# Query loads with four tokens in a row per partition, in a chunked attention block that feeds a GELU MLP

## The chip, the core and the metric

The kernel runs on one core of a Trainium2 chip. The metric is the device time of one execution in microseconds (us). Three runs of the kernel before gave 198.75, 198.85 and 199.21 us, median 198.85 us. A difference of 0.2% of that is 0.4 us.

## The reference

Inputs are q, k and v of shape (4, 8, 768, 64): batch, heads, tokens, head dimension, all fp32, with one decay `lam` per head, and two MLP weights of 512 x 2048 and 2048 x 512. The attention walks over blocks of 64 tokens. The result of the attention is laid out as 3072 tokens of 512 features and goes through the MLP.

```python
for b in range(nb):                       # 12 blocks of 64 tokens
    intra = einsum('bhic,bhjc->bhij', qb, kb) * Dmask      # lam ** (i - j), i >= j
    intra = einsum('bhij,bhjd->bhid', intra, vb)
    inter = einsum('bhid,bhde->bhie', qb * lam_pow, kv_state)   # lam ** (i + 1)
    out[:, :, sl] = intra + inter
    kv_state = lam ** 64 * kv_state + einsum('bhsd,bhse->bhde', kb * rev_pow, vb)
x = out.transpose(0, 2, 1, 3).reshape(3072, 512)
result = gelu_tanh(x @ w_in) @ w_out
```

## The kernel before, in words

**Steps.** The attention is cut into 24 steps. A step is 256 tokens of 4 heads, of one batch row; even steps take heads 0 to 3, odd steps heads 4 to 7 of the same tokens. `load_step` (L60) brings q, k and v of a step in three DMAs of 256 KB: a partition p holds tokens 2p and 2p + 1 of each of the four heads, so each DMA packet is two tokens of 64 fp32 values, 512 bytes. In SBUF the order is (head, token of the pair, dimension). With this layout, the upper and the lower 64 partitions are the two halves (chunks, called `c`) of 128 tokens.

**Decays.** The block's decay is put on the operands: q is multiplied by `dq` (a power of lam by the token's place, from -63 upward within a chunk of 128 tokens) and v by `dv`, its reciprocal; the mask then only has to be 0 or 1. The powers are made once at the start: lam is spread over all partitions by a small transpose on TensorE (L207) and copied to `lam_bc` (L209); GpSimd raises it to `pos` (two `pow` instructions of 128 x 4, L216); VectorE makes the second token of each pair with `odd` (L224), and the reciprocals with `inverse` (L227). Seven squarings on VectorE (L221) give lam to the power of 128 for the state's decay, which four small copies on ScalarE (`chunk_decay`, L229) place into `lumask` and `lamu`.

**One step.** `cast_q` (L277) multiplies q by dq and writes fp16, on VectorE (on GpSimd for step 3). `cast_k` (L290) converts k on ScalarE. `scale_v` (L264) multiplies v by dv on GpSimd. Steps 0 to 7 are transposed on TensorE (`stage_t`, L309) and copied out of PSUM; in steps 0 to 3 ScalarE copies q's half and VectorE k's (L325, L326). From step 8 on `transpose_dma` (L299) does it with a DMA transpose on SP's queue. `scores` (L344) multiplies k with q into PSUM, `causal` (L356) multiplies by the mask on VectorE, `products` (L365) or `burst` (L415) forms the state update, the masked scores times v, and q times the state. `x_out` (L475) copies the result on ScalarE to `xT` in token order. `update` (L491) advances the state on VectorE and spreads it into `u` on GpSimd.

**The MLP** is cut into pieces by `queue_group` (L544), which wait in a list called `filler`. `fill(n)` runs the next n pieces, so the order of TensorE's work is written out by hand at the end of the function (L930 to L1132): attention steps with MLP pieces between them. Every instruction is pinned to its place in program order, and each engine works through its own instructions in order.

**Loads.** All loads but `lam` and v of step 0 are issued by SP, in one queue: steps 0 to 2, q and k of step 3, the first half of the first block of w_in (`load_win(0, 0)`, L88), v of step 3, the second half, the rest of w_in, w_out (L96), then steps 4 to 8. Later steps are loaded where the program says so. Each of the q, k, v buffers has four copies, so a load also waits until the step four before it has been used. DMA transposes and output stores share SP's queue with the loads.

**The start.** Until the MLP's first pieces can run, TensorE has little to do, and `idle` (L177) gives it dummy products. The first MLP pieces are `mm1_part` (L832, matmuls at L838). They run in an order that follows the arrival of the data: the first two feature blocks of x against the first half of w_in, then the second two against the second half, whose casts are at L108 on ScalarE and L110 on VectorE.

```python
    for s in range(3):
        load_step(s)
    load_step(3, "qk")
    load_win(0, 0)
    load_step(3, "v")
    load_win(0, 1)
```

Of the kernel before, what the change touches and what calls it, by code (L numbers as in the profile page):

```python
# [15 lines left out]
def kernel(  # L16
# [43 lines left out]
    def load_step(s, names="qkv"):  # L60
        b, r = divmod(s, 2 * NSB)
        sb, half = divmod(r, 2)
        ts = ld32.setdefault(s, [])
        for nm, src in (("q", q), ("k", k), ("v", v)):
            if nm not in names:
                continue
            t = ld.tile([P, HH, 2, D], FP32, tag=nm + "32", name=f"{nm}32_{s}")
            rows = src[b, half * HH : (half + 1) * HH, sb * SB : (sb + 1) * SB, :]
            queue = nc.scalar if (nm, s) == ("v", 0) else nc.sync
            pin(queue.dma_start(out=t[:].rearrange("p h j d -> p h (j d)"),  # L70
                                in_=rows.rearrange("h (p j) d -> p h (j d)", j=2)))
            ts.append(t)
# [104 lines left out]
    def idle(n, wide=0):  # L177

        t = ps_M.tile([P, 512], FP32, tag="M", name="idle")
        for dt, w in [(FP32, wide)] * (wide > 0) + [(mybir.dt.bfloat16, 512)] * n:  # L180
# [3 lines left out]
    pos = const.tile([P, H], FP32)  # L184
    nc.gpsimd.iota(pos[:], pattern=[[0, H]], base=-63, channel_multiplier=2,
                   allow_small_or_imprecise_dtypes=True)
    nc.gpsimd.tensor_scalar(pos[64:128], pos[64:128], 128.0, None, ALU.subtract)

    rel = otp.tile([P, 2, 2, 64], FP32, tag="o32", name="rel")
    nc.gpsimd.iota(rel[:], pattern=[[-1, 2], [1, 2], [2, 64]], base=0, channel_multiplier=-2,  # L190
                   allow_small_or_imprecise_dtypes=True)
    ident = const.tile([P, P], FP16)
# [14 lines left out]
    pin(nc.tensor.transpose(lam_ps[:], lam_in[:].to_broadcast([H, P]), ident32[:]))  # L207
    lam_bc = const.tile([P, H], FP32)
# [3 lines left out]
    dq = const.tile([P, H, 2], FP32)  # L212
    dv = const.tile([P, H, 2], FP32)
    halves = [slice(hf * HH, (hf + 1) * HH) for hf in range(2)]
    for hs in halves:
        pin(nc.gpsimd.tensor_tensor(dq[:, hs, 0], lam_bc[:, hs], pos[:, hs], ALU.pow))  # L216
    sq = [lam_bc] + [const.tile([P, H], FP32, name=f"sq{i}", tag=f"sq{i}") for i in range(7)]
    lamu = const.tile([P, H // 2], FP32)

    def square(i):  # L220
        pin(nc.vector.tensor_tensor(sq[i + 1][:], sq[i][:], sq[i][:], ALU.mult))  # L221

    def odd(hs):
        pin(nc.vector.tensor_tensor(dq[:, hs, 1], dq[:, hs, 0], lam_bc[:, hs], ALU.mult))  # L224

    def inverse(hs):
        pin(nc.vector.reciprocal(dv[:, hs], dq[:, hs]))  # L227
# [9 lines left out]
    for i in range(7):  # L237
        square(i)
    odd(halves[0])


# [10 lines left out]
    def decay(t, s):  # L252
        hs = halves[s % 2]
        return t[:, hs, :].unsqueeze(3).to_broadcast([P, HH, 2, D])

# [21 lines left out]
    def cast_q(s):  # L277
# [4 lines left out]
        pin(q_eng.tensor_tensor(wide(tq), q32[:], decay(dq, s), ALU.mult))  # L282
        if s == 0:
            inverse(halves[0])
            odd(halves[1])
            inverse(halves[1])
# [22 lines left out]
    def stage_t(s):  # L309
# [7 lines left out]
        for i, t in enumerate((tq, tk)):  # L317
            to = Tps[i] if s < 4 else Tps[:, i]
            for hp in range(2):
                for j in range(2):  # L320
                    pin(nc.tensor.transpose(to[:, j, hp, :], t[:, j, 2 * hp : 2 * hp + 2, :],
                                            ident[:]))
# [18 lines left out]

    Ss = {}

    def scores(n):  # L344
        o = qkT[n]
        Sps = [ps_M.tile([P, 2, 2, P], FP32, tag="M", name=f"S{hl}") for hl in range(2)]
        for hp in range(2):
            for jk in range(2):
                for hl, c in TILES:
                    pin(nc.tensor.matmul(  # L350
                        Sps[hl][half64(c), hp, jk, :], o[half64(hl), 1, jk, hp, half64(c)],
                        o[half64(hl), 0, :, hp, half64(c)], start=True, stop=True,
# [12 lines left out]
    def products(n, s, banks=None, evacuate=True):  # L365
# [37 lines left out]
        for c in range(2):  # L403
# [3 lines left out]
            for hp in range(2):  # L407
                pin(nc.tensor.matmul(OK[c][:, hp * P : hp * P + P], u[:, hp].rearrange("p l d -> p (l d)"),  # L408
                                     o[:, 0, :, hp, half64(c)], start=False, stop=True,
# [5 lines left out]
    def burst(ns, ss, *mix, ahead=None):  # L415
# [39 lines left out]
        for i, s in enumerate(ss):  # L455
            for c in range(2):
# [3 lines left out]
                for hp in range(2):  # L460
                    pin(nc.tensor.matmul(O[c][:, i, hp, :], u[:, hp].rearrange("p l d -> p (l d)"),  # L461
                                         qTs[i][:, 0, :, hp, half64(c)], start=False, stop=True,
# [12 lines left out]
    def x_out(s, OK, second=None):  # L475
# [5 lines left out]
        for c in range(2):  # L481
            d = dst[:, :, c * P : (c + 1) * P].rearrange("p hp (t j) -> p hp j t", j=2)
            o = OK[c][:, 0:256].rearrange("p (hp j t) -> p hp j t", hp=2, j=2)
# [447 lines left out]
    prep(0)  # L931
    stage_t(0)
    chunk_decay()
# [227 lines left out]
```

## Time and profile before

| What | Value |
|---|---|
| median of three runs | 198.85 us (198.75 to 199.21) |
| the profiled execution | 198.79 us |
| its span in the profile | 197.0 us, so 1.79 us lie around the span |
| TensorE (PE) busy | 191.2 us, 97% |
| VectorE (DVE), ScalarE (ACT), GpSimd (POOL) busy | 149.0, 121.1, 74.4 us |
| DMA packets | 62,810, of 38.13 MB |
| granted TensorE clock | full speed throughout |
| q load | 24 issues of 256 KB, median 4.9 us from issue to landing |

PE is the TensorE matmul queue, PEld its weight loads, SP the engine that only issues DMAs. "L70" is line 70 of the kernel; a line such as `L70` may stand for several loads, so they are told apart by tile. The profile's chain of work goes back from the last instruction to whatever released each one. Busy time of PE includes the dummy products of the first microseconds, and says nothing by itself on whether a stage could start sooner.

### The profile page before, as it was taken

How to read it: one execution, taken by the hardware profiler on the slowest of the kernel's cores; microseconds unless marked ns; L12 is line 12 of the kernel's file. 1: busy time of each engine (PE TensorE's matmuls, PEld its weight loads, DVE VectorE, ACT ScalarE, POOL GpSimd, SP SyncE). 2: the span in 40 equal slices, each digit the busy share in tenths (PEclk: the TensorE clock that was granted, in tenths of full speed). 3: DMA queues.
4: the chain of work that ended last, by engine and by line, in shares of the span. 5: the costliest groups of instructions: out<-in, count | busy, mean ns of one | idle time of the engine just before them, and what ended most of it. 6: DMA issues, size and time to landing. Idle time of an engine off the chain costs nothing.

```text
span 197.0 us, 5913 instructions
## 1 busy us (share of the span) xinstructions
PE 191.2 (97%) x2431; PEld 140.1 (71%) x2431; DVE 149.0 (76%) x291; ACT 121.1 (61%) x249; POOL 74.4 (38%) x85
## 2 busy tenths in 40 slices
PE   8979999999999999999999999999999999999993
PEld 2556544446888888654688764578888888888882
DVE  4797722889999889859999927999656987487620
ACT  3663878357874685686845378844867746679221
POOL 6594213457554931169754517165002030002000
PEclk9999999999999999999999999999999999999999
DMA  5999999999999999999996998400211300020205
GB/s 167 292 324 384 387 383 386 300 285 297 259 220 248 257 333 231 213 238 288 226 294 132 274 310 202 92 7 0 53 67 42 107 6 2 0 110 29 77 19 198
DMA packets 62810, 38.13 MB, mean 194 GB/s; under 512 B 18624, under 2 KB 55744, under 8 KB 62784
## 3 DMA queue, kind: packets, MB, share of 16 engines
q1 hardware_dynamic: 62240, 37.50, 74.3%
q8 instruction: 19, 0.31, 0.7%
q10 hardware_dynamic: 544, 0.26, 0.5%
q14 instruction: 7, 0.06, 0.1%
HBM read 27.26 MB, written 6.29 MB: 170 GB/s over the span
## 4 chain that ended last, share of the span: by engine, by line
PE 89%; SPq 4%; DMA 4%; ACT 0%; issue 0%
PE Hps L561 25%; PE MX L640 18%; PE MY L640 9%; PE HX L739 7%; PE O2ps L576 7%; PE MW L640 4%; DMA wi<-in_moe_w_in_dram 4%; SPq L70 4%; PE HY L739 4%; PE S L350 3%; PE Hps L838 3%; PE HW L739 2%; PE OK L408 2%; PE O L461 1%; PE O L436 1%; PE OK L399 1%
## 5 line engine op out<-in xcount | busy, mean ns | idle before, releaser
L561 PE MATMUL Hps<-xT,w_in 128*128 128x512 f16 (+1 forms) x288 | 50.5, 332 | 0.0
L513 POOL TENSOR_TENSOR u<-t,lumask 128x256 f16<-128x256 f32 x40 | 30.9, 788 | 40.7 <-DVE t L506 27.0
L561 PEld LDWEIGHTS <-w_in 128*128 128x128 f16 x288 | 27.9, 98 | 19.1
L565 ACT ACTIVATE gT<-Hps 128x512 f16<-128x512 f32 x56 | 33.5, 598 | 11.6 <-PE Hps L561 11.1
L360 DVE TENSOR_TENSOR PT<-S,mask 128x512 f16<-128x512 f32 x48 | 30.3, 680 | 7.8 <-PE S L350 7.8
L266 POOL TENSOR_TENSOR v<-v,dv 128x512 f16<-128x512 f32 x24 | 28.7, 1197 | 15.2 <-DMA v<-in_v_dram 14.0
L640 PEld LDWEIGHTS <-gs 128*128 128x128 f16 x320 | 31.2, 98 | 3.6
L640 PEld LDWEIGHTS <-gT 128*128 128x128 f16 x240 | 23.3, 98 | 3.2 <-ACT gT L565 0.2
L640 PE MATMUL MX<-w_sum,gs 128*128 128x256 f16 x160 | 21.4, 273 | 0.0
L692 POOL TENSOR_TENSOR o<-u,q 128x512 f32<-128x512 f32 (+1 forms) x5 | 6.3, 1252 | 36.7 <-ACT u L657 36.7
L282 DVE TENSOR_TENSOR qk<-q,dq 128x512 f16<-128x512 f32 x23 | 19.1, 833 | 0.8 <-DMA q<-in_q_dram 0.7
L295 ACT ACTIVATE qk<-k 128x512 f16<-128x512 f32 x23 | 14.4, 625 | 7.4 <-DMA k<-in_k_dram 7.3
L610 DVE TENSOR_TENSOR gs<-gT 128x1024 f16<-128x1024 f16 (+1 forms) x24 | 16.9, 711 | 1.6 <-ACT gT L565 1.6
L576 PE MATMUL O2ps<-w_out,gT 128*128 128x512 f16 x64 | 14.6, 379 | 0.0
L487 ACT ACTIVATE xT<-OK 128x256 f16<-128x256 f32 x26 | 9.9, 452 | 7.0 <-PE OK L408 6.5
L739 PEld LDWEIGHTS <-ws 128*128 128x128 f16 x128 | 12.5, 98 | 1.6 <-issue 0.2
L487 ACT ACTIVATE xT<-O 128x256 f16<-128x256 f32 x22 | 8.0, 461 | 5.8 <-PE O L461 4.9
L657 ACT ACTIVATE u<-MX 128x256 f32<-128x256 f32 x18 | 6.9, 384 | 7.4 <-PE MX L640 7.3
L576 PEld LDWEIGHTS <-gT 128*128 128x128 f16 x64 | 6.1, 98 | 6.6
L350 PEld LDWEIGHTS <-qkT 64*64 64x64 f16 x384 | 6.0, 106 | 6.8 <-issue 3.6
L640 PE MATMUL MY<-w_out,gs 128*128 128x256 f16 x80 | 10.7, 273 | 0.0
L753 DVE COPY u<-HX 128x512 f32<-128x512 f32 x8 | 5.5, 688 | 6.8 <-ACT gT L757 4.3
(98 smaller groups left out, 318.4 us busy)
## 6 DMA issues: line engine op xcount, KB each, us to landing
q<-in_q_dram SPq DMA_DIRECT2D x24, 256.0 KB, 4.9
k<-in_k_dram SPq DMA_DIRECT2D x24, 256.0 KB, 5.0
v<-in_v_dram SPq DMA_DIRECT2D x23, 256.0 KB, 5.2
out_dram<-o SPq DMA_DIRECT2D x23, 256.0 KB, 4.3
wo<-in_moe_w_out_dram SPq DMA_DIRECT2D x4, 1024.0 KB, 9.4
wi<-in_moe_w_in_dram SPq DMA_DIRECT2D x4, 512.0 KB, 7.1
wi<-in_moe_w_in_dram SPq DMA_DIRECT2D x2, 1024.0 KB, 12.5
v<-in_v_dram ACTq DMA_DIRECT2D x1, 256.0 KB, 4.3
```

What stands on the lines that cost most here:

```text
L266: pin(nc.gpsimd.tensor_tensor(wide(tv[:]), ld32[s][2][:], decay(dv, s), ALU.mult))
L282: pin(q_eng.tensor_tensor(wide(tq), q32[:], decay(dq, s), ALU.mult))
L295: pin(nc.scalar.activation(out=wide(tk), in_=k32[:], func=AF.Copy))
L360: pin(nc.vector.tensor_tensor(t[:, hl].rearrange("p b c d -> p b (c d)"), Sps[:].rearrange("p b c d -> p b (c d)"), mask[:].unsqueeze(1).t ...
L487: pin(nc.scalar.activation(out=d, in_=o, func=AF.Copy))
L513: pin(nc.gpsimd.tensor_tensor(u[:], state[half][:].unsqueeze(2).to_broadcast([P, 2, 2, D]), lumask[:, 2 * half : 2 * half + 2, :].unsqueez ...
L561: pin(nc.tensor.matmul(by_block(Hps[:, i, :]), w_in16[:, c, f * P : (f + 1) * P], x(c), start=(c == 0), stop=(c == NC - 1)))
L565: pin(nc.scalar.activation(out=dst, in_=Hps[:], func=AF.Gelu_apprx_tanh))
L576: pin(nc.tensor.matmul(O2[tau][0][:], gT[:, f % HF, f // HF, tau * P : (tau + 1) * P], w_out16[:, f, :], start=(n == 0), stop=(n == NF - 1)))
L610: pin(nc.vector.tensor_tensor(g_rows(m, i), g_rows(a, i), g_rows(b, i), op))
L640: pin(nc.tensor.matmul(dst, lhsT, rhs, start=(opens and i == 0), stop=(closes and i == HF - 1), skip_group_check=True))
L739: pin(nc.tensor.matmul(dst[:, i, :], w_in_block(a, slice(c, c + 1), slice(f * P, f * P + P))[:, 0], x_block(b, slice(c, c + 1))[:, 0], sta ...
```

## The change

q is no longer loaded two tokens to a partition, but four. Its tile becomes (2 heads, 4 tokens, 64), and it is loaded in two DMAs of 64 partitions each: partitions 0 to 63 get heads 0 and 1 of the step, partitions 64 to 127 heads 2 and 3, with tokens 4p to 4p + 3. A packet is 1 KB, a DMA 128 KB. k and v stay as they were.

The rest follows from the new order. `dq` becomes (half, head pair, 4 tokens) and needs lam per partition half (`lam_q`) and its own position column `pos_q`; `dv` is no longer a reciprocal of dq but has a `pow` of its own with `pos_v`, and a multiplication by 1/lam. The mask's `iota` (a ramp of integers) follows the new order of queries. `stage_t` transposes the q tile in its new blocks; `queries` picks the columns of a chunk as four runs of 32 instead of two of 64; `x_out` writes its columns four apart instead of two apart. The seven squarings, which stood in one row ahead of the first `cast_q`, are spread: one before it, three after it, and three after `stage_t(0)`. The second half's `pow` for dv and the multiplication behind it go to GpSimd, after step 0's v.

```diff
+            if nm == "q":
+                t = ld.tile([P, 2, 4, D], FP32, tag=nm + "32", name=f"{nm}32_{s}")
+                for hp in range(2):
+                    pin(nc.sync.dma_start(
+                        out=t[64 * hp : 64 * hp + 64].rearrange("p l j d -> p l (j d)"),
+                        in_=rows[2 * hp : 2 * hp + 2].rearrange("l (p j) d -> p l (j d)", j=4)))
+                ts.append(t)
+                continue
...
-    nc.gpsimd.tensor_scalar(pos[64:128], pos[64:128], 128.0, None, ALU.subtract)
...
+    for i in range(1, 4):
+        r = slice(32 * i, 32 * i + 32)
+        pin(nc.vector.tensor_scalar(pos_q[r], pos_q[r], 128.0 * i, None, ALU.subtract))
+    pin(nc.vector.tensor_scalar(pos_v[64:128], pos_v[64:128], 128.0, None, ALU.add))
...
+    for hp in range(2):
+        r = slice(64 * hp, 64 * hp + 64)
+        pin(nc.vector.tensor_copy(out=lam_q[r], in_=l4[r, :, hp, :]))
...
-    for hs in halves:
-        pin(nc.gpsimd.tensor_tensor(dq[:, hs, 0], lam_bc[:, hs], pos[:, hs], ALU.pow))
+    def pow_q(hf):
+        pin(nc.gpsimd.tensor_tensor(dq[:, hf, :, 0], lam_q[:, hf, :], pos_q[:].to_broadcast([P, 2]),
+                                    ALU.pow))
+    def pow_v(hs):
+        pin(nc.gpsimd.tensor_tensor(dv[:, hs, 0], lam_bc[:, hs], pos_v[:].to_broadcast([P, HH]),
+                                    ALU.pow))
+    pow_q(0)
+    pow_v(halves[0])
+    pow_q(1)
...
+    def later_q(hf):
+        pin(nc.vector.tensor_tensor(dq[:, hf, :, 1], dq[:, hf, :, 0], lam_q[:, hf, :], ALU.mult))
+        pin(nc.vector.tensor_tensor(dq[:, hf, :, 2:4], dq[:, hf, :, 0:2],
+                                    lam_q2[:, hf, :].unsqueeze(2).to_broadcast([P, 2, 2]), ALU.mult))
+    def later_v(hs, eng):
+        pin(eng.tensor_tensor(dv[:, hs, 1], dv[:, hs, 0], inv[:, hs], ALU.mult))
...
-    for i in range(7):
-        square(i)
-    odd(halves[0])
+    pin(nc.vector.tensor_tensor(lam_q2[:], lam_q[:], lam_q[:], ALU.mult))
+    square(0)
+    later_q(0)
...
         if s == 0:
-            inverse(halves[0])
-            odd(halves[1])
-            inverse(halves[1])
+            pin(nc.vector.reciprocal(inv[:], lam_bc[:]))
+            later_v(halves[0], nc.vector)
+            later_q(1)
+            for i in range(1, 4):
+                square(i)
...
+    def queries(o, r, hp, c):
+        return o[r, 0].rearrange("p a b t -> p (a b) t")[:, :, 64 * hp + 32 * c : 64 * hp + 32 * c + 32]
...
-            d = dst[:, :, c * P : (c + 1) * P].rearrange("p hp (t j) -> p hp j t", j=2)
+            d = dst[:, :, c * P : (c + 1) * P].rearrange("p hp (t j) -> p hp j t", j=4)
...
     prep(0)
+    pow_v(halves[1])
+    later_v(halves[1], nc.gpsimd)
     stage_t(0)
+    for i in range(4, 7):
+        square(i)
     chunk_decay()
```

## The prediction

> **What bounds the kernel now.** I read the slices first, then the chain of waits in order of time, then the stages in which the chain was not on TensorE. A time is called measurable here if it differs by over 0.2%, 0.4 us. In the page's slices (PE: TensorE busy, DMA: busy share of the 16 DMA engines, in tenths):
>
> ```profile
> PE   8979999999999999999999999999999999999993
> DMA  5999999999999999999996998400211300020205
> ```
>
> After the start TensorE has no gap, so from about 20 us to 193.8 us the time is fixed matmul work; but the DMA engines are full over the first half as well. What decides the start is in the chain (start us, us, what):
>
> ```profile
> 8.47 0.83 SPq L94
> 9.35 0.47 SPq L70
> 9.81 0.04 issue
> 9.86 7.88 DMA wi<-in_moe_w_in_dram
> 17.74 0.02 issue
> 17.77 0.42 ACT w_in L108
> 18.19 0.05 issue
> 18.24 1.13 PE Hps L838 x8
> ...
> 41.61 0.12 PE OK L385 x8
> 41.73 0.33 PE Tps L321 x4
> 42.06 0.03 issue
> 42.09 0.40 PE Tps L321 x4
> ```
>
> TensorE's unbroken work starts at 18.24 us, behind the second half of the first w_in block, which landed at 17.74 us. Ahead of it in SP's queue stand q of steps 0 to 3. And at 42.09 us the transposes of step 5's k start 0.03 us late: ScalarE converts that k at 41.40 to 42.03 after waiting 3.5 us for its DMA. So a later stream of loads meets the path a second time there, with six q loads before it. The stages by microsecond (last columns: granted clock, DMA share, GB/s):
>
> ```profile
> 10.00:11.00 1.00, 1.00 (x46) 0.67 (x35) 1.00 (x2) 0.74 (x2) 1.00 (x2) 1.00 1.22 290
> 16.00:17.00 1.00, 1.00 (x12) 0.86 (x10) 1.00 (x3) 0.10 (x1) 0.53 (x1) 1.00 1.05 385
> 17.00:18.00 1.00, 0.89 (x22) 0.53 (x20) 0.49 (x2) 0.23 (x1) 0.51 (x1) 1.00 1.06 391
> ```
>
> The engines' DMA share is over 1 in each. The q, k, v packets of 512 B move at 290 GB/s, the w_in packets of 2 KB at 385 to 391. The third number after the comma is VectorE: full from 7 to 17 us. It is the second chain of the start:
>
> ```profile
> 4.54 0.15 DVE L224 TENSOR_TENSOR dq<-dq,lam_bc 128x4 f32<-128x4 f32 x1
> 6.77 0.42 DVE L326 COPY qkT<-Tps 128x512 f16<-128x512 f16 x1 [0.96 <-PE Tps L321]
> 15.97 1.28 DVE L360 TENSOR_TENSOR PT<-S,mask 128x512 f16<-128x512 f32 x2
> 17.77 0.43 DVE L110 CAST w_in<-wi 128x512 f16<-128x512 f32 x1 [0.51 <-DMA wi<-in_moe_w_in_dram]
> ```
>
> Its only slack before 18 us is 0.51 us ahead of the last line and about 0.1 us near 12.5 us.
>
> **What the Trainium skill says.** "SBUF — State Buffer", Door 1: The DMA port swizzle: partitions 0 to 63 reach 8 of the 16 DMA ports; it gives 196 GB/s measured for 64 partitions at 1 MiB, against 328 for 128, and a ceiling of about 218 GB/s. The same page, "Can I just issue two DMAs to hit both halves?": no, two such DMAs together gained 6% over one. No load of before has 64 partitions, so its trace can't tell. "DMA: Bandwidth & Descriptors", Why small descriptors are slow (HBM only): a fixed cost per packet, some 3 cycles beside 32 B per cycle. The trace agrees in sign and shows more: 2-KB packets are 1.33 times as fast as 512-B ones.
>
> **The change part by part.**
>
> *Packets.* 256 KB at 290 GB/s take 0.904 us, 32 packets on each engine, 28.2 ns a packet. At 388 GB/s they take 0.676 us, 8 packets, 84.5 ns. A straight line between them (9.4 ns plus 0.0367 ns per byte) puts a 1-KB packet at 47.0 ns; 16 of them are 0.752 us. So by packets alone a q load gains 0.15 us.
>
> *Half the partitions.* If each half is held to the page's rates, 256 KB take 1.20 us at 218 GB/s or 1.34 us at 196: 0.30 to 0.43 us more. The two halves stand back to back in the same engines' queues between full-width loads; one engine may already write the other half, or k, while its partner finishes, which gives some of it back. I take +0.2 us per q load, inside the bounds -0.15 and +0.43, and nearer to the slow one since the page's two-DMA test found little overlap. This number is the prediction.
>
> *Where it counts.* Four q loads stand before the w_in half of 17.74 us: +0.8 us at 18.24 us, whole, since TensorE waits for this DMA already. Six stand before step 5's k: +1.2 us at 42.09 us, of which 0.8 is paid; cover there is 0.03 us, so the rest, 0.4, is paid too. Step 6's k (landed 43.7 us, transposed at 45.23) has over 0.5 us of cover, step 7's (46.3 us, transposed at 50.17) 3 us. Later steps go through DMA transposes that land 2 to 5 us ahead of their scores, but for step 16: issued at 88.2 us, landed about 92.7, scores near 93.9. There the slower q loads and one more issue in front can cost 0 to 0.5 us; I take 0, as the queue's delay does not add up over the steps where SP waits for casts (24.2 us in its waits).
>
> *Issues.* 24 more on SP, 0.45 to 0.5 us each. Ahead of the w_in half it is four, 2.1 us. They hide: from 3.97 us on SP's issues of 0.5 us are stretched to 0.8 to 1.6 us by full queues, 2.7 us in all before 9.86. Step 0's k is issued 0.53 us later (1.78 us instead of 1.25); behind it in the queue the engines still have q and v of step 0, so its landing (5.35 us) moves by the q load's cost, not by 0.53. Without that cover it would cost up to 0.5 us at the first transpose.
>
> *The setup.* VectorE gains four tiny position subtractions and additions before 1.5 us, where it waits (one GpSimd instruction of 0.33 us goes away). After lam's transpose come two copies for lam_q ahead of lam_bc, about 0.1 us each. GpSimd then has three `pow` before step 0's v, not two. A `pow` of 128x4 takes 1.02 us; a subtraction of 64x8 takes 0.33, so I read 0.3 fixed and 0.18 per column: 0.66 us for the new 128x2, bounded by 0.4 and 1.02. They end at 3.4 + 0.66 + 1.02 + 0.66 = 5.7 us, before 5.85 where v was scaled: no cost. The first q cast keeps its 4.7 us (squares no longer stand ahead of it; the second `later_q` does). Then VectorE does reciprocal, `later_v`, two of `later_q` and three squares from 5.2 to 6.7 us, hidden in the 0.96 us wait before 6.77. The last three squares (0.195 us each from start to start, 0.59 us) fall behind that copy, into the full stretch: every VectorE step to 17 us moves by 0.6. ScalarE's four `chunk_decay` copies wait for the last square, until 7.8 instead of 6.83, and behind them in its queue k of step 1 is converted at 8.65, not 7.71; its transposes move by 0.6, which VectorE's delay covers. At the end 0.6 meets a slack of 0.51 on VectorE; on TensorE scores of step 3 (15.37), eight MLP pieces and the state product move by 0.6 and end at 18.45 instead of 17.89. With unchanged DMA, the MLP's second part would start at 18.45: +0.2 us. With DMA 0.8 later it costs nothing.
>
> *Layouts.* `stage_t`, `queries`, the mask and the casts keep their counts and columns. Runs of 64 cost nothing today (eight 128-column products of q and state take 0.55 us, four 0.33: 55 ns each), so runs of 32 are put at 0. A strided `x_out` takes 0.45 us against 0.38 for a plain 128x256 copy; the wider stride may add 0 to 0.07 us, 48 times on ScalarE, which is idle 39% of the time; in the start, four in a row (14.43 to 16.11) have 0.5 us before their use. Zero.
>
> *Sum.* 0.8 + 0.4 = +1.2 us, on the profiled execution's 198.79 (span 197.0 plus 1.79 around it), which lies 0.06 below the median: 200.0 us.
>
> **Rivals.**
> (a) VectorE and ScalarE set the start: `pow` costs 1.02 whatever its width, so the third ends at 6.45; VectorE stands at `later_q(1)` and all squares and the copy of 6.77 come 0.6 later, 1.2 in all. Less the slack, +0.8 at 18.24 us, with q loads about as before: 199.6. For it: VectorE full from 7 to 17 us. Against: a per-element price for `pow` is more natural.
> (b) Offset: ports don't bind, q loads gain 0.15 us, and the w_in half lands 0.6 earlier; but the setup's 0.2 takes the place of the wait, and steps 4 and 5 no longer wait. +0.1: 198.9.
> (c) Faster: the same gain, and the moved squares fall into gaps. The w_in half would land at 17.1 us; TensorE could then start as soon as its own queue allows, at 17.89 instead of 18.24, 0.35 us earlier, and a little is won at 42 us: 198.4. It decides from the point where q loads take under 0.85 us and the added VectorE work under 0.1 us net.
> (d) The loads don't become 1-KB packets: the page would show 62,810 packets again instead of 62,810 - 24 x 256 = some 56,700. The slices of the access pattern speak against it.
>
> **Chances.** Forecast (q loads 0.05 to 0.43 us dearer: 199.1 to 201.4): 0.55. (a) 0.15, (b) 0.17, (c) 0.13 (with (d) under 0.01 inside them). Range 198.4 to 201.0: about 0.1 is left out above (page's full price and a stall at step 16) and 0.1 below. The forecast's own range is 199.1 to 201.4. Faster by over 0.2% is (c), 0.13; within is (b) and the forecast's mildest end, 0.21; slower is the rest, 0.66.
>
> **What would show it.** In the stages from 5 to 12 us: GB/s under 290 shows the ports, over 300 the packets. The first w_in half-block should land near 18.5 us and the L838 matmuls behind it start near 19.0. Step 5's k should be waited for by ScalarE until about 42.5. VectorE's second cast of q should start near 7.7, and `chunk_decay` near 7.8. If L838 restarts at or before 18.3 us, the q load's price is wrong; if it is late while the w_in half landed at 17.7, (a) holds; if TensorE shows a new wait near 93 us, the later part is wrong.

## The result, and the profile after

The changed kernel takes 206.87 us against 198.82 us of the kernel before on the same chip: ratio 1.0398, 95% interval 1.0343 to 1.0453, slower by about 8 us. The forecast was 200.0 us, range 198.4 to 201.0. Of its six executions (205.28 to 210.11 us), two count as slow, being over 1.5% above the fastest (208.63 and 210.11 us); they are left out of the median and the ratio, and slow executions of the experiments below likewise. The profiled execution took 208.63 us (span 206.8), so the lags read from it run up to 9.8 us rather than 8.

The page's slices (5.2 us each) and its line on packets:

```profile
PE   8597999998899999969999999999999999999993
PEclk9979999999999999999999999999999999999999
DMA  4999999999999999999999998970022200020205
...
DMA packets 57053, 38.14 MB, mean 184 GB/s; under 512 B 19009, under 2 KB 49985, under 8 KB 57025
```

The packets are close to the forecast (57,053 against some 56,700), so q does arrive in 1-KB pieces. But TensorE now has a hole in the second slice, a granted clock of 0.7 in the third, and a hole near 90 us, the 6 in PE's row. The stages (last columns: granted clock, DMA share, GB/s):

```profile
4.00:5.00 1.00, 1.00 (x3) 0.27 (x2) 0.33 (x2) 0.00 (x0) 1.00 (x2) 1.00 0.81 163
6.00:7.00 1.00, 0.40 (x4) 0.23 (x4) 0.86 (x5) 0.00 (x0) 0.20 (x1) 1.00 1.13 187
10.00:11.00 1.00, 1.00 (x2) 0.51 (x3) 1.00 (x3) 0.93 (x5) 0.00 (x0) 0.50 1.21 233
17.00:18.00 1.00, 0.94 (x22) 0.47 (x19) 1.00 (x3) 1.00 (x2) 0.80 (x2) 1.00 1.11 381
```

From 10 to 11 us the same engines that moved 290 GB/s before move 233, with the same share of 1.2. From 4 to 5 us they are not even full. The w_in packets (17 to 18 us) move at 381 GB/s, near the 385 to 391 of before: whatever slows the loads is tied to the q, k, v stream. TensorE's own lines, in order of time (start us, us, then the idle time before it and what ended it):

```profile
8.48 0.40 PE L363 MATMUL Tps<-ident,qk 128*128 128x128 f16 x4 [1.68 <-ACT qk L336]
...
19.59 2.02 PE L882 MATMUL Hps<-xT,w_in 128*128 128x256 f16 x16
21.54 0.32 PE L429 MATMUL OK<-v,qk 64*64 64x64 f16 x16
21.80 0.94 PE L882 MATMUL Hps<-xT,w_in 128*128 128x256 f16 x7
```

The first wait is not at the w_in half but at the transposes of step 0's k: 6.10 us before, 8.48 now. Before, they were the last four of this line, which also holds the four of q:

```profile
5.67 1.06 PE L321 MATMUL Tps<-ident,qk 128*128 128x128 f16 x8
```

The L882 line of 21.80 us is the MLP's second part that stood at 18.24; it has no wait of its own in front, it comes after late work. But the w_in half is late too: it landed at 20.80 us, 17.74 before, and ScalarE's casts of it ended near 21.5 us, under 0.3 us before TensorE came to it. Further on there are two more waits, at k of step 5 (42.09 us before) and at a piece of the MLP's second product (80.94 before), each in its own stretch of TensorE's timeline:

```profile
47.34 0.40 PE L363 MATMUL Tps<-ident,qk 128*128 128x128 f16 x4 [0.71 <-ACT qk L336]
```

```profile
89.86 1.03 PE L684 MATMUL MX<-w_sum,gT 128*128 128x256 f16 x8 [1.75 <-ACT u L701]
```

The second of these lines was, in the kernel before:

```profile
80.94 1.04 PE L640 MATMUL MX<-w_sum,gT 128*128 128x256 f16 x8
```

ScalarE shows what it stands behind in the changed kernel:

```profile
88.91 0.63 ACT L336 ACTIVATE qk<-k 128x512 f16<-128x512 f32 x1 [3.15 <-DMA k<-in_k_dram]
89.44 0.37 ACT L701 ACTIVATE u<-MX 128x256 f32<-128x256 f32 x1
```

A late k load holds ScalarE in its conversion for 3.15 us; the copy `u` (here a partial sum of the MLP), next in ScalarE's order, has nothing to do with k but waits too, and TensorE with it. The lag of the same matmul against the kernel before is 2.4 us at step 0's k, 3.6 at the MLP's second part, 4.0 until 39 us, 5.3 at 42, 7.0 at 62, 8.9 at 81 and 9.8 at the end.

### The profile page after: what moved, and what is told of

Read it like the earlier page. It is cut to its first block, busy times and chain, and to the rows that moved or that the text cites. A ratio compares the mean times of both kernels' runs of the same rounds, so it can differ in the third digit from the quotient of the medians.

```text
span 206.8 us, 5967 instructions
## 1 busy us (share of the span) xinstructions
PE 193.9 (94%) x2429; PEld 140.5 (68%) x2431; DVE 150.3 (73%) x300; ACT 131.2 (63%) x249; POOL 73.4 (35%) x88
## 2 busy tenths in 40 slices
DMA packets 57053, 38.14 MB, mean 184 GB/s; under 512 B 19009, under 2 KB 49985, under 8 KB 57025
## 4 chain that ended last, share of the span: by engine, by line
PE 49%; DMA 26%; DVE 12%; ACT 5%; SPq 4%; issue 2%; DVEq 0%; ACTq 0%
PE MX L684 14%; PE Hps L605 10%; DMA k<-in_k_dram 8%; DMA q<-in_q_dram 8%; DMA wi<-in_moe_w_in_dram 7%; PE HX L783 6%; PE MY L684 6%; DVE gs L654 4%; DMA v<-in_v_dram 3%; PE HY L783 3%; PE MW L684 3%; SPq L72 2%; DVE PT L404 2%; ACT xT L531 2%; PE S L394 2%
## 5 line engine op out<-in xcount | busy, mean ns | idle before, releaser
L557 POOL TENSOR_TENSOR u<-t,lumask 128x256 f16<-128x256 f32 x40 | 30.0, 764 | 38.9 <-DVE t L550 30.1
L609 ACT ACTIVATE gT<-Hps 128x512 f16<-128x512 f32 x56 | 32.2, 605 | 6.9 <-PE Hps L605 6.4
L684 PEld LDWEIGHTS <-gT 128*128 128x128 f16 x240 | 23.3, 98 | 5.1 <-issue 1.9
L531 ACT ACTIVATE xT<-OK 128x256 f16<-128x256 f32 x26 | 17.1, 792 | 6.8 <-PE OK L452 5.2
L736 POOL TENSOR_TENSOR o<-u,q 128x512 f32<-128x512 f32 (+1 forms) x5 | 5.8, 1165 | 36.7 <-ACT u L701 36.7
L531 ACT ACTIVATE xT<-O 128x256 f16<-128x256 f32 x22 | 13.9, 805 | 4.8 <-PE O L505 4.2
L684 PE MATMUL MX<-w_sum,gT 128*128 128x256 f16 x80 | 10.4, 272 | 1.7 <-ACT u L701 1.7
L550 DVE SCALAR_TENSOR_TENSOR t<-t,lamu,OK 128x64 f32<-128x64 f32 x36 | 8.4, 275 | 3.7 <-ACT xT L531 1.5
```

The lines of the kernel that those rows point to most:

```text
L531: pin(nc.scalar.activation(out=d, in_=o, func=AF.Copy))
L557: pin(nc.gpsimd.tensor_tensor(u[:], state[half][:].unsqueeze(2).to_broadcast([P, 2, 2, D]), lumask[:, 2 * half : 2 * half + 2, :].unsqueez ...
L609: pin(nc.scalar.activation(out=dst, in_=Hps[:], func=AF.Gelu_apprx_tanh))
L684: pin(nc.tensor.matmul(dst, lhsT, rhs, start=(opens and i == 0), stop=(closes and i == HF - 1), skip_group_check=True))
```

## The experiments

Each edit is made in the kernel before, unless it says otherwise; times are medians, ratios against the kernel before on the same chip, brackets behind a ratio its 95% interval.

### The parts alone

*The load.* Only q's load becomes two DMAs of 64 partitions.

```diff
+                for hp in range(2):
+                    pin(nc.sync.dma_start(out=t2[64 * hp : 64 * hp + 64],
+                        in_=rows[2 * hp : 2 * hp + 2].rearrange("l (p j) d -> p l (j d)", j=4)))
```

> The kernel before, with only q's load changed: two DMAs of 64 partitions, 1-KB packets, into the same tile (the four heads' values then stand in another order, so the queries are mixed up; all else is as before). Theory A, the half-width loads are the cause: over half of the 8.7 us, 204 to 206 us, with the first w_in half landing some 2.5 us later than before and waits for q and k near 42 us. Theory B, the four-apart columns of the output copy are the cause: 200.0 to 200.5 us, as I forecast for the load. Theory C, the moved setup is the cause: under 200.5 us too.

Measured: 207.02 us, ratio 1.0409 (1.0366 to 1.0452), +8.2 us. This one part costs as much as the whole change. The first w_in half landed at 19.65 us, 1.9 later than before (2.5 expected). Two stages of the steady stream of loads:

```profile
41.00:42.00 1.00, 1.00 (x7) 0.41 (x6) 0.67 (x1) 0.15 (x1) 0.17 (x1) 1.00 1.21 195
...
44.00:45.00 1.00, 1.00 (x6) 0.29 (x3) 0.38 (x2) 0.00 (x0) 0.71 (x1) 1.00 1.19 211
```

The mean from 40 to 52 us, first in the kernel before, then with the load alone:

```profile
40.00:52.00 12.00, 11.97 (x193) 7.79 (x192) 10.95 (x22) 8.63 (x16) 8.50 (x9) 1.00 1.13 290
```

```profile
40.00:52.00 12.00, 11.10 (x130) 5.86 (x127) 7.78 (x16) 6.08 (x10) 5.05 (x6) 1.00 1.20 229
```

That is 229 GB/s against 290, with the engines no less busy. A step's 768 KB take 3.43 us in place of 2.71: +0.72 per q load.

*The columns.* `x_out` writes four apart, as in the change.

```diff
-            d = dst[:, :, c * P : (c + 1) * P].rearrange("p hp (t j) -> p hp j t", j=2)
+            d = dst[:, :, c * P : (c + 1) * P].rearrange("p hp (t j) -> p hp j t", j=4)
```

> The kernel before, with only the output copy's columns written four apart instead of two (tokens of the result in another order). The copy should take 0.79 us instead of 0.46, as in the changed kernel's page. Theory A: ScalarE is idle 39% of the time, so at most +1 us, 199 to 200 us. Theory B: over half of the loss, 203 us or more. Theory C: under 199.5 us.

Measured: 200.57 us, ratio 1.0084 (1.0055 to 1.0113), +1.7 us. In the changed kernel's page the copy takes 0.79 to 0.81 us; before it took 0.452 and 0.461:

```profile
L531 ACT ACTIVATE xT<-OK 128x256 f16<-128x256 f32 x26 | 17.1, 792 | 6.8 <-PE OK L452 5.2
...
L531 ACT ACTIVATE xT<-O 128x256 f16<-128x256 f32 x22 | 13.9, 805 | 4.8 <-PE O L505 4.2
```

*The rest* (setup, decays, layouts, mask), that is the change with the old load and the old columns:

```diff
-                for hp in range(2):
...
+                pin(nc.sync.dma_start(out=t[:].rearrange("p l j d -> p (l j d)").rearrange("p (h x) -> p h x", h=HH),
+                                      in_=rows.rearrange("h (p j) d -> p h (j d)", j=2)))
```

> The changed kernel with the old load (one DMA of 256 KB with 512-B packets, into q's tile, so the queries are mixed up) and the columns two apart again: what stays is the setup of the decays, the moved squares and the new query slices. Theory A and theory B: 199.0 to 199.6 us (VectorE's 0.6 us and chunk_decay's wait at the start, less slack). Theory C: 202 us or more.

Measured: 199.69 us, ratio 1.0042 (1.0032 to 1.0052), +0.86 us. Its timeline shows why:

```profile
5.83 1.04 POOL L302 TENSOR_TENSOR v<-v,dv 128x512 f16<-128x512 f32 x1
5.90 0.99 DVE L255 TENSOR_TENSOR dq<-dq,lam_q 128x2 f32<-128x2 f32 x1 [0.21 <-POOL dq L235]
```

VectorE's multiply of 128x2 takes 0.15 us where GpSimd is not at work on v (the setup with another order, below); here it starts while GpSimd scales v and ends with it. The squares, the second q cast (8.29 us, 7.11 before) and `chunk_decay` (8.41, 6.83 before) follow late. The Trainium skill, "SBUF — State Buffer", Who interferes with whom, says that a VectorE instruction with two SBUF inputs contends with a GpSimd instruction that reads SBUF; this line agrees. The three parts sum to 10.8 us, the change cost about 8: together the parts cost less than one by one, so the waits of one plausibly cover those of another.

### Is it the packets, the width or the count?

*1-KB packets without half width* (one DMA of 128 partitions, other tokens):

```diff
+                wide_rows = src[b, half * HH : half * HH + 2, lo : lo + 2 * SB, :]
+                pin(nc.sync.dma_start(out=t2, in_=wide_rows.rearrange("l (p j) d -> p l (j d)", j=4)))
```

> The kernel before, with q loaded in 1-KB packets but in one DMA over all 128 partitions (512 tokens of two heads instead of 256 of four, so the queries are other ones; bytes are the same). Theory A1, the half-width form of the DMA is the cause and not the packet or the order in HBM: the load now gains, 197.9 to 198.8 us. Rival: 1-KB packets of q are slow in themselves in this program: over 202 us.

Measured: 198.63 us, ratio 0.9986 (0.9976 to 0.9996). The rate at 40 to 50 us is 306 GB/s: 2.57 us a step, 0.14 less than 2.71. The packets are a small gain in the rate, of the forecast's size; 0.2 us in time.

*Half width with 512-B packets* (q in two DMAs of 64 partitions, tile content as before):

```diff
+                for c in range(2):
+                    pin(nc.sync.dma_start(
+                        out=t[64 * c : 64 * c + 64].rearrange("p h j d -> p h (j d)"),
+                        in_=rows[:, 128 * c : 128 * c + 128].rearrange("h (p j) d -> p h (j d)", j=2)))
```

> The kernel before, with q loaded in two DMAs of 64 partitions, the packets still 512 B, every value where it was. Theory A1: about what the load alone cost, 206 to 208 us. Rival, the 1-KB packets: 199 to 200 us.

Measured: 208.66 us, ratio 1.0511 (1.046 to 1.0562). The cut costs; no packet size needs to change for that. From 4 to 5 us the engines' share is 1.15 here, against 0.81 in the changed kernel, with the same times of issue.

*The same bytes in two DMAs of 128 partitions* (by head pairs):

```diff
+                for g in range(2):
+                    hs = slice(2 * g, 2 * g + 2)
+                    pin(nc.sync.dma_start(out=t[:, hs].rearrange("p h j d -> p h (j d)"),
+                                          in_=rows[hs].rearrange("h (p j) d -> p h (j d)", j=2)))
```

> The kernel before, its q load cut into two DMAs by head pairs, each into all 128 partitions with 512-byte packets (128 KB each); nothing else differs, so against the run of the split alone (two DMAs of 64 partitions, same packets, 208.66 us) only the width of the DMA does. Theory (the width slows the engines, the second issue costs what the tiny DMA cost): 201 to 203.5 us, rate near 280 GB/s at 40 to 52 us. Rival (it is the count of DMAs alone): 207 to 209.5 us, rate near 230. Rival (only the issue of half-width DMAs is long, a second full-width one is short): 199 to 200.5 us.

Measured: 199.30 us, ratio 1.0012 (0.9992 to 1.0033): not told apart from no change. Same count of DMAs, same size of packets, same bytes as the run before it, and 9.4 us less. What differs is the width, and with it which rows of the source a DMA takes (all tokens of two heads instead of half the tokens of four). My theory (201 to 203.5 us) fell in the time, though its rate came (282 GB/s from 40 to 52 us); the rival came, by which only the issue of half-width DMAs is long. SP's issues at the start (start us, us for all), half width first, then full width:

```profile
0.73 1.40 SPq L71 DMA_DIRECT2D q<-in_q_dram  x2
2.18 0.60 SPq L77 DMA_DIRECT2D k<-in_k_dram  x1
```

```profile
0.74 0.96 SPq L72 DMA_DIRECT2D q<-in_q_dram  x2
1.75 0.46 SPq L77 DMA_DIRECT2D k<-in_k_dram  x1
```

The x2 line is two issues: at half width each takes 0.60 to 0.74 us of SP, and the full-width k behind one 0.60; at full width each is 0.46 to 0.48. And the stages of the full-width run from 41 us, against 195 and 211 GB/s above:

```profile
41.00:42.00 1.00, 1.00 (x29) 0.54 (x27) 1.00 (x3) 0.39 (x1) 0.00 (x0) 1.00 1.07 286
...
44.00:45.00 1.00, 1.00 (x42) 0.60 (x40) 0.39 (x2) 0.88 (x3) 0.68 (x1) 1.00 1.15 299
```

*Four DMAs of 128 partitions* (64 KB each): more SP time than the half-width pair, at full width.

```diff
-                for g in range(2):
-                    hs = slice(2 * g, 2 * g + 2)
+                for g in range(4):
+                    hs = slice(g, g + 1)
```

> The kernel before with its q load cut into four DMAs by head, each into all 128 partitions (64 KB each): SP then issues for about 2.4 us a step, more than the 1.85 of the two half-width DMAs and k. Theory (the half-width DMAs cost through the engines, SP's issue time is of little account): 199 to 202 us, rate at 40 to 52 us 270 or more. Rival (SP's issue time is what costs): 208 us or more. In between: both have a part.

Measured: 210.13 us, ratio 1.0555 (1.0515 to 1.0595). Its emptiest microseconds of the steady stream:

```profile
40.00:41.00 1.00, 0.72 (x4) 0.10 (x2) 0.66 (x1) 0.43 (x1) 0.44 (x1) 1.00 0.53 146
41.00:42.00 1.00, 0.91 (x10) 0.62 (x11) 0.51 (x3) 0.00 (x0) 0.11 (x1) 1.00 0.53 149
```

My theory, that SP's time is of little account, fell. Here the engines starve (share 0.53 in these stages, 0.85 and 242 GB/s on average from 40 to 50 us) while SP issues back to back, 3.0 us a step from 41.7 to 50 us, more than the 2.7 us that the engines need. It lags by 2.1 us at 15 us, 3.9 at 59, 7.4 at 81 and 9.7 at 87: most is lost from 58 us on, where DMA transposes and output stores share SP's queue. So two full-width DMAs (about 2.1 us of SP a step) hide and four do not. The half-width pair (about 2.5 us) lies between them, with engines that are slower as well; on which side it would lie by its issues alone, no run shows.

*A further tiny DMA ahead of each q load*, meant as the issue alone, half width (128 packets of 16 B, shown here), and then full width (`out=extra[:]`, 256 packets):

```diff
+                extra = ld.tile([P, 2, 4], FP32, tag="extra", name=f"extra_{s}")
+                pin(nc.sync.dma_start(out=extra[0:64],
+                    in_=rows[2:4].rearrange("l (p j) d -> p l (j d)", j=4)[:, :, 0:4]))
```

> The kernel before, with its q load whole, and ahead of each one more DMA of 64 partitions that moves 16 bytes to each of two places of a partition (2 KB in all; the squares share two buffers to make room). It costs SP an issue, and one more transfer in flight[...]. Theory A2, SP's issue time is the cause (0.6 us for each half, and step 0's k issued late): at least half of the load's 8.2 us, over 203 us. Theory A3, the ports are the cause: 199.0 to 200.5 us.

> The kernel before with one more tiny DMA ahead of each q load, as in the run of the issue alone (3.9 us), but into all 128 partitions (16-byte packets, 4 KB). Theory (what costs is that the DMA fills half the partitions, bytes or none): 198.8 to 200 us, the load behind it issued in 0.48 us instead of 0.59. Rival (any further DMA of that kind costs, by its many small packets): 202 to 203.5 us.

Measured: 202.74 us (1.0157 to 1.0239) at half width, between its two theories, and 202.72 us (1.0153 to 1.0214) at full. The width theory of this pair fell: it makes no difference. At full width the tiny DMA is issued in 0.45 us, as any other, and two full-width DMAs cost nothing that can be told; so its 3.9 us are not SP's issue time either. (To make room, the squares of lam share two buffers in both runs; their chain takes 1.17 us as before.) What is left is the 128 or 256 packets of 16 B, in a way that isn't traced: in the third stage of the long streams below, 64 packets of 32 B ahead of each q cost 0.03 us a step, 287 GB/s against 290. For the change this pair says nothing.

### How much do half-width loads cost by themselves?

Loads alone, no attention computed: short stages of one form each, then 12 loads of whole q, k, v against 12 with q halved; ahead of them, copies out of PSUM with several strides.

```python
    stage("half1k", [(half1k, q, n, {}) for n in range(8, 16)])
    ...
    stage("mixb", [(full512, (q, k, v)[i % 3], 16 + i // 3, {}) for i in range(12)])
    stage("mixa", [(half1k if i % 3 == 0 else full512, (q, k, v)[i % 3], 20 + i // 3, {})
                   for i in range(12)])
```

> No attention and no MLP: streams of loads one after another, each stage waiting for the one before, with ScalarE and VectorE copies from PSUM in several output orders beside them; the output is zeros. If half-width transfers are bound by their ports (theory A): alternating halves of 128 KB run near 200 GB/s and so does a stream that stays on the lower half, full-width 1-KB packets near 350, full-width 512-B ones near 290; halves with 2 KB a partition stay near 200. If it is the issue time on SP instead: SP's issues follow one another without a gap at 0.63 us per 128 KB, and the stage with 256-KB halves is faster. If packets win over ports: alternating halves at 300 GB/s or more. Copies: one apart 0.38 us, two apart 0.46, four apart 0.79; eight apart 0.8 if it is a fixed cost per separate word, more if it grows; reading PSUM in steps and writing in a row tells whether the cost is on the writing side.

Measured: halves in a stream of their own, two 128-KB DMAs per 256 KB, are bound by SP, 0.65 us from issue to issue, 201 GB/s. Halves of 256 KB each land every 1.11 to 1.17 us once there is a backlog, about 230 GB/s, against about 295 for full width; that is a little above the 196 to 218 that the prediction had used. In the mixed stream twelve loads took 14.12 us with q halved and 13.28 with q whole: +0.21 us per q load, the forecast's figure, though SP's issues (2.49 us a step there) have a part in so short a stream. In a row, a ScalarE copy of 128x256 takes 384 ns; writing fp16 two apart 456, four apart 737, eight apart 1302; reading in steps and writing in a row 384.

Twenty-four steps each into 72 buffers, `whole` and then `halves` (the fences' last three columns: granted clock, DMA share, GB/s):

> No attention is computed, the output is zeros: three stages of 24 steps (72 loads of 256 KB each into buffers of their own, so that nothing but SP and the DMA engines limits them): q, k and v whole; q in two DMAs of 64 partitions; q whole behind one more DMA of 64 small packets. Theory (half-width DMAs slow the engines once a backlog has built up): whole 2.65 us a step (295 GB/s), halves 3.3 to 3.5 us a step, tiny 2.7 to 2.9. Rival (halves only cost what the short stream showed): 2.85 us a step. Rival (SP's issue time bounds the halves): the landing follows the issue by under 3 us all the way, at 2.3 us of SP a step.

```profile
12.00:60.00 48.00, 0.00 (x0) 0.00 (x0) 1.00 1.20 290
95.00:145.00 50.00, 0.00 (x0) 0.00 (x0) 1.00 1.19 263
```

A step takes 2.99 us instead of 2.71, +0.28 per q load: nearer to the rival's 2.85 than to the 3.3 to 3.5 of my backlog theory, which fell. The same with four compute engines at work on tiles of their own (a VectorE product, one or two ScalarE copies, a GpSimd product and three matmuls, 64 to 68 times in each stage):

> No attention is computed, the output is zeros: the long streams of loads again (whole, then q in two half-width DMAs), this time with VectorE, ScalarE, GpSimd and TensorE working all the while on tiles of their own in SBUF. Theory (in the kernel the half-width DMAs lose more because the compute engines use SBUF at the same time): whole stays near 290 GB/s, halves fall from 263 to 225 to 240 GB/s, 512-byte packets from 35 to over 40 ns. Rival (compute has no part in it): halves stay at 260 to 266 GB/s. If whole falls too, the contention is not the halves' own.

```profile
12.00:60.00 48.00, 39.80 (x185) 17.91 (x184) 47.04 (x29) 45.69 (x74) 45.75 (x29) 0.97 1.17 291
135.00:196.00 61.00, 43.15 (x199) 19.32 (x197) 59.77 (x37) 58.08 (x93) 58.17 (x37) 0.89 1.14 245
```

Whole loads move as fast beside the compute engines (291), halved ones slower in this run (245): 3.21 us a step, +0.50. That is between the theory and its rival, and it rests on one profile each, from two different chips. The Trainium skill, "SBUF — State Buffer", Who interferes with whom, says that a DMA never contends with a compute engine; for whole loads the run agrees, for halved ones the 263 against 245 GB/s speak against it, without showing it. The kernel's own +0.72 is reached by neither; the last 0.2 is open.

### What lies beside the load

*The clock*: the load alone with seven filler products of 512 columns ahead of step 0 in place of two (`idle(7, 512)`).

> The load alone (q in two half-width DMAs in the kernel before, queries mixed up), with seven in place of two filler matmuls of 512 columns ahead of step 0's transposes, so that TensorE is busy while it waits for the late q and k. Theory (TensorE's clock of 0.50 from 8 to 14.8 us is a consequence that adds about 1 us of the 4 us at the start): the clock stays above 0.9 and the time is near 206 us, against 207.0. Rival (the clock costs nothing, loads decide all of it): 207.0 within 0.5. If the fillers themselves delay the first transposes: 207.5 or more.

Measured: 209.59 us (206.71 to 209.74), not below the 207.02 of the load alone. The clock did stay full from 8 to 15 us, and TensorE's lag at the end of the start was 2.8 us in place of 4.0; by 42 us it was 5.5 and at 81 us 10.6. What was gained at the start was lost again by 42 us, so in this run a full clock there bought nothing that stayed. More could hardly be gained there: TensorE comes to the MLP's second part at 20.98 us, 0.2 us after the casts of the w_in half, which had waited 1.4 us for its DMA. The time lies in the range of the expectation's third case, but the fillers don't delay step 0: k's transposes come at 7.73 us, 7.85 in the load alone.

*The setup with another order*: squares (and the reciprocal of lam) ahead of the first q cast, GpSimd's `pow` for q's second half before that for v, and `later_v` behind `later_q(1)`.

```diff
     pow_q(0)
-    pow_v(halves[0])
     pow_q(1)
+    pow_v(halves[0])
...
+    for i in range(7):
+        square(i)
     later_q(0)
```

> The setup alone (old load, columns two apart; queries mixed up, as in the run of the rest alone), with the squares put ahead of the first q cast's multiplies again and GpSimd's order pow q 0, pow q 1, pow v 0, so that VectorE's small multiply no longer stands beside GpSimd's scaling of v. Theory (that multiply's 0.99 us behind GpSimd and the squares behind it are the 0.86 us): 198.8 to 199.1 us, second q cast near 7.5 us instead of 8.29. Rival (GpSimd's longer pow or the wider four-token cast is the cause): 199.5 to 199.8 us.

Measured: 199.30 us, ratio 1.0025 (1.0015 to 1.0034), against 1.0042 for the rest alone. The small multiply is short again and the second q cast back where it was:

```profile
5.97 0.15 DVE L255 TENSOR_TENSOR dq<-dq,lam_q 128x2 f32<-128x2 f32 x1
...
7.11 0.95 DVE L320 TENSOR_TENSOR qk<-q,dq 128x512 f16<-128x512 f32 x1
```

But only about half of the 0.86 us came back, and the intervals just touch. GpSimd now scales v of step 0 at 6.47 us, 5.85 before, after 0.64 us of waiting for VectorE's `later_v`; the last of the three `pow` had ended at 5.84. The second q cast starts on time but takes 0.95 us instead of 0.68, beside that scaling. So the long multiply beside GpSimd was likely a part and this longer cast another; the rest is open.

*The copies reading in steps and writing in a row*, in the kernel before, then in the changed one:

```diff
-            d = dst[:, :, c * P : (c + 1) * P].rearrange("p hp (t j) -> p hp j t", j=2)
-            o = OK[c][:, 0:256].rearrange("p (hp j t) -> p hp j t", hp=2, j=2)
+            d = dst[:, :, c * P : (c + 1) * P].rearrange("p hp (t j) -> p hp t j", j=2)
+            o = OK[c][:, 0:256].rearrange("p (hp j t) -> p hp t j", hp=2, j=2)
```

> The kernel before, with the output copy reading PSUM in steps of 64 elements and writing tokens in a row, instead of reading in a row and writing two apart; result unchanged. From the copies measured by themselves (0.384 us against 0.456): 0.07 us less for each of 48 copies on ScalarE. If ScalarE's copies of the start stand on the path: 198.4 to 198.7 us; if ScalarE is covered everywhere: 198.8, no difference.

> The changed kernel with x_out's copies reading in steps of four and writing in a row (the same values), so that a copy costs near 400 ns in place of 790. Theory (the loads decide, the slow copies mostly stand in time that is waited anyway): 206 to 207.3 us, so 0.2 to 1.5 us back. Rival (the parts add up): 205.8 us, 1.7 back. Rival (the copies stand in the path of every late k cast): 204.5 us or less.

Measured: 198.81 us (0.999 to 1.0012) in the kernel before, no difference; 205.97 us (1.0316 to 1.0417) in the changed kernel, 0.9 us under it, with intervals that overlap; theory and rival can't be told apart by it. With the setup's order mended too (both edits, in the changed kernel):

> The changed kernel with both other parts mended: x_out writes in a row, and the squares and pows in the order of the setup run (squares ahead of the first q cast, pow q 0, pow q 1, pow v 0). What is left is the load in two half-width DMAs. Theory: 206 to 207.3 us, the load's own 8.2 us less little. Rival (parts add up): 205 us. Rival (the setup's lock on VectorE sets the start): 205.5 and the first q cast earlier by over 1 us.

Measured: 206.94 us (1.0343 to 1.0431). Three kernels with the half-width load and less or none of the rest (this one, the one above, the load alone) lie at 206.0 to 207.0 us, the changed kernel at 206.9. The columns and the setup, worth 1.7 and 0.86 us alone, are worth at most 0.9 us beside it, which the intervals don't tell from nothing.

### A load that can't be full width so easily

The changed kernel with q's two DMAs cut the other way, one head of each pair into all 128 partitions:

```diff
+                for l in range(2):
+                    pin(nc.sync.dma_start(out=t[:, l].rearrange("p j d -> p (j d)"),
+                        in_=rows.rearrange("(hp l) (p j) d -> l hp p (j d)", hp=2, j=4)[l]))
```

> The changed kernel, with q's two DMAs cut the other way: each fills one head's four tokens in all 128 partitions (128 packets of 1 KB), in place of all of 64 partitions; the tile's content, and all else, is the same. Theory (half the partitions is what costs: a longer issue on SP and slower DMA engines): an issue costs near 0.47 us instead of 0.60 to 0.74, the rate at 40 to 52 us goes back from 229 to over 270 GB/s, and what stays is the second issue, the columns and the setup: 201.5 to 204 us. Rival (two DMAs where there was one is what costs, whatever their width): 205.5 to 208 us, as the change. Rival (the columns and the setup are most of it): also 205.5 or more.

Measured: 288.99 us, ratio 1.4555, far from every theory.

```profile
7.00:8.00 1.00, 0.00 (x0) 0.00 (x0) 0.00 (x0) 0.00 (x0) 0.00 (x0) 0.92 0.14 49
8.00:10.00 2.00, 0.00 (x0) 0.00 (x0) 0.00 (x0) 0.00 (x0) 0.00 (x0) 0.50 0.14 46
```

A share of 0.14 is two of sixteen engines, at 23 GB/s each. The source's outermost dimension is the head pair, of size 2. The Trainium skill, "DMA: Bandwidth & Descriptors", Rules for kernel authors, says that an outermost dimension of fewer than 16 confines a DMA to that many engines; the share agrees. The run therefore doesn't test the width; the cut by head pairs does.

## Why the prediction was wrong, step by step

*Packets: right.* 0.15 us less per q load from packets was the estimate; 0.14 was measured at full width, and the packet count held within 1%. Rival (d) is out.

*Half the partitions: the sign right, the size wrong.* The sign that was named for the ports, under 290 GB/s in the start's stages, came (233). But "+0.2 us per q load" was mis-sized. In an isolated stream it is 0.21 to 0.28, but 0.72 in the kernel (229 against 290 GB/s), beyond my upper bound of 0.43. That bound priced q's own 256 KB at the skill's rates for 64 partitions. The packet records show that this is not where it ends: k's and v's full-width 512-B packets took 44 ns at the median from 40 to 52 us in the load run, 31 in the kernel before. What is in flight beside the halves is slower too, so the price had to be set on the step's 768 KB.

*Where it counts: too few places.* I charged two, 18.24 and 42.09 us, and took "the later part" at 0. At 18.24 the lag was 3.6 instead of 0.8 us: the w_in half landed 3.1 us late (1.9 with the load alone), so that path was charged rightly and its price was off two- to fourfold. At step 5's k the lag rose by 1.3 us, not 0.4. From there to 94 us it grew by 4.2 more. The failing thought was that the queue's delay "does not add up over the steps". It does: each step's loads need 3.4 us of the engines instead of 2.7 while they stream. From 58 us on SP's own queue is dense, and the four-DMA run, full width but 3.0 us of SP a step, lost most of its time in that same stretch; that the halves lose it there for the same reason is argued from this likeness, not tested. The wait that was thought possible, at step 16's scores near 93 us, did not come as such: they start at 103.05 us with the lag TensorE already had. The new wait at 89.86 us stands before a matmul that ran at 80.94 us before, behind an earlier k.

*Issues: "they hide" failed.* The count was right to hide: at full width 24 more issues cost between -0.2 and 0.7 us. But these take 0.60 to 0.74 us, not 0.45 to 0.5, and the k behind them 0.60. Step 0's k was to move "by the q load's cost, not by 0.53". It was issued at 2.18 instead of 1.25 us and landed at 7.77 us instead of 5.35; the engines' share of 0.81 from 4 to 5 us would fit a lack of issued loads, but with the same issue times and 512-B halves it was 1.15. The w_in half was issued at 11.83 us instead of 9.86 (10.42 with two DMAs at full width). So TensorE waited first for k, which I had not charged; but the w_in half, on which I had put the start's whole sum, was late by over 3 us as well. The two lie close together. In the load alone TensorE came to the MLP's second part at 22.04 us, over 1 us after the w_in half's casts; in the 512-B split it came at 20.77 us, 0.2 us after casts that had waited 1.6 us for the DMA. Where only k was about 1 us late (two DMAs at full width, w_in half on time at 17.63 us), TensorE's lag was back to 0.2 us by 18 us.

*The setup: the amount small, the mechanism missed.* `pow` of 128x2 took 0.71 us (0.66 estimated), which rules out rival (a)'s price; and (a)'s sign, a w_in half landed at 17.7 us, did not come. But "+0.2" became 0.86 alone: `later_q(1)`, "hidden in the 0.96 us wait", met GpSimd's scaling of v, and its multiply took 0.99 us instead of 0.15; in the changed kernel it is the other multiply of the pair, 1.03 us at 6.83.

*Layouts: half right.* Runs of 32 cost nothing: sixteen score products take 0.42 us as before. `x_out` "0 to 0.07 us" was wrong: +0.34. I had drawn a line from one point, a row against a stride of two, where the step from two to four is the large one. Alone it is +1.7 us, so "Zero", reasoned from a ScalarE that "is idle 39% of the time", was wrong as well: in ScalarE's fixed order each copy also delays what TensorE waits for; in that run's timeline TensorE stands 0.27 us before 21.85 us for `xT`.

*Shown, and open.* Shown: the half width of the two DMAs is the cause of practically the whole loss (alone +8.2 us; the same cut at full width +0.4, not told from nothing). With it come slower engines (rate) and longer issues. How the 8 us split between the two isn't settled: within the kernel no run had the slower engines without the longer issues. Nor is it settled why halves lose 0.72 us a step in the kernel, 0.28 alone and 0.50 beside busy engines.

## What to carry to other kernels

Before cutting a load, write down two budgets per step: SP's time for all its issues, and the engines' time for all bytes at the mixed rate; here a second full-width DMA of 128 KB, with both under the step, cost nothing that can be told, and four DMAs, with SP's time above it, cost 11 us. The two budgets aren't everything: tiny DMAs kept within them and cost 3.9 us. If a load must be cut, cut it along the free dimension, not along the partitions, as far as these runs go: the same bytes in the same count of DMAs cost 9.4 us more as two times 64 partitions. A late load that feeds one conversion delays every later instruction on that engine, so follow the engine's order, not only the data.

## What the runs showed of the hardware

- At the start of the kernel, issuing a DMA of 64 partitions took SP 0.60 to 0.74 us, one of 128 partitions 0.43 to 0.51; a full-width one behind a half-width one 0.60.
- In a stream of q, k, v loads, q in halves of 64 partitions brought the rate from 290 GB/s to 263 in a long stream by itself and to 229 in the kernel; the full-width 512-B packets beside the halves took 44 ns instead of 31.
- ScalarE copies of 128x256 from PSUM to fp16 slow with the write stride (384, 456, 737, 1302 ns for 1, 2, 4, 8 apart); stepping on the PSUM read side took no longer (384).
- With TensorE idle for 1.7 us near 7 us, its granted clock was 0.50 from 10 to 13 us.
- A DMA of 128 or 256 packets of 16 B ahead of each q load cost 3.9 us over the kernel; q as two DMAs of 128 KB instead of one of 256 cost 0.4, not told from nothing.
